# An FFT filter and a bilinear layer on one core: x's seven blocks and w_out's blocks 1024 bytes apart, used from 12 bytes behind the tile's begin

## The chip, the core and the metric

The kernel runs on one core of one Trainium2 chip. The metric is the device time of one launch in microseconds. Before the change it is 2662.38 us, the median of three runs (2661.9 to 2662.65). The profile is of one more execution, which took 2663.02 us.

A core has five engines that matter here: TensorE (PE; its weight loads are a row of their own, PEld), VectorE (DVE), ScalarE (ACT), GpSimd (POOL) and SyncE (SP), which here issues most DMAs. A matmul has a *stationary* operand, 128 x 128 weights that are loaded first, and a *moving* operand, which streams past them from SBUF, one column at a time, and gives one column of the result in PSUM each.

## The reference

x is 8 x 3072 x 256. Along the 3072 positions it is filtered in the frequency domain, and the result goes through a bilinear layer of 1536 hidden features:

```python
X = np.fft.rfft(x, axis=1)                  # 8 x 1537 x 256
Y = X * (filt_r + 1j * filt_i)[None]
y = np.fft.irfft(Y, n=3072, axis=1)         # float32
t = y.reshape(8 * 3072, 256)
a, b = t @ w_a, t @ w_b                     # 256 -> 1536 each
out = (a * b) @ w_out                       # 1536 -> 256
```

## The kernel before, in words

The FFT is done as two short transforms with a store to DRAM between them, forward and back, all as matmuls. Batch 0 goes through it in a stage of its own at the start, in an order written out by hand (FIRST). After that the kernel streams: while TensorE does the bilinear layer of batch b, the transforms of batch b+1 are put in between at places given by slots (`at(slot, ...)`). The schedule is manual; each engine runs its instructions in the order in which the code issues them.

The bilinear layer runs over 8 batches, 6 chunks of 512 tokens in each (c), and 6 pairs of hidden blocks in each chunk (p; two of the 12 blocks of 128 features). All its operands are split in a high and a low part, rounded to the float32r type, and a product is three matmuls: high weights by high x, low weights by high x, high weights by low x (L644, L645, L646 in `term`). The products a and b take Strassen's seven terms instead of eight: the chunk of x is kept as seven blocks of 256 columns (four quadrants and three sums, `x_parts`), in the tiles xoh (high) and xol (low), two buffers of each, taken in turn by the chunks. One `term` is six matmuls with one x block as the moving operand of 256 columns, and weights w as the stationary one. A pair has seven terms, 42 matmuls.

The product of a and b is made on VectorE (g), rounded on ScalarE (gh, L652), its remainder taken on GpSimd (gl, L653). `project` then multiplies it by w_out: gh and gl are the stationary operands, and a 256-column block n = 2p + f of w_out's high and low parts, woh and wol, is the moving one (L663, L664, L665). A pair has eight such triples, 24 matmuls. So a pair has 66 matmuls with an x block or a w_out block as the moving operand, and there are 8 x 6 x 6 = 288 pairs.

Where the blocks lie is what the change touches. In SBUF a block of 256 float32 takes 1024 bytes in each partition. Before, the x blocks stand XW = 261 elements (1044 bytes) apart, and the whole tile is used from 0 bytes behind its begin in even chunks and from SHIFT = 2 elements (8 bytes) in odd ones; w_out's blocks stand WW = 257 elements (1028 bytes) apart. The program that is built puts every one of these tiles at a multiple of 64 bytes. So the address at which a block begins, modulo 16 bytes, is

- x block i (0 to 6): 4 i modulo 16 in even chunks (0, 4, 8, 12, 0, 4, 8) and 4 i + 8 in odd ones (8, 12, 0, 4, 8, 12, 0);
- w_out block n: 4 n modulo 16, that is 0 or 8 for f = 0 and 4 or 12 for f = 1.

This address modulo 16 of the moving block is called its *class* below: class 0, 4, 8 or 12. Stationary operands (w, gh, gl) all begin at multiples of 64.

The blocks are written by ScalarE and GpSimd: xoh at L628, xol at L629 (four pieces of a chunk, of one or two blocks each), woh at L307, wol by the helper on L316.

Of the kernel before, what the change touches and what calls it, by code (L numbers as in the profile page):

```python
# [9 lines left out]
F32 = mybir.dt.float32  # L10
F32R = mybir.dt.float32r
# [7 lines left out]
B, S, D, DFF = 8, 3072, 256, 1536  # L19
N1, N2 = 128, 24  # L20
NB = 32
NF = DFF // 128
NP = NF // 2
NC = 6
NI = 12
NJ = 16
NFT = 4
XW, SHIFT, WW = 261, 2, 257
ODD = [1, 5, 7, 11, 13, 17, 19, 23]

PAIRS = [(0, 2), (4, 6), (8, 10), (12, 14), (16, 18), (20, 22), (3, 9), (15, 21), (1, 5), (7, 11), (13, 17), (19, 23)]
# [177 lines left out]
def fft_filter_bilinear_kernel(ctx: ExitStack, tc, x, filt_r, filt_i, wa, wb, wo, s1c, gc, fc, fl, ic, sc, s1f, ff, fi, out):  # L209
# [3 lines left out]
    def pool(name, bufs=1, space=None):  # L213
        kw = {} if space is None else {"space": space}
        return ctx.enter_context(tc.tile_pool(name=name, bufs=bufs, **kw))

    const = pool("const")
    p2 = pool("p2", 2)


    edge = ctx.enter_context(tc.tile_pool(name="edge", bufs=1, side="right"))
    few = edge.tile([128, 24], F32, name="few")
    sct, cut = few[:, 0:2], few[:, 2:4]


# [23 lines left out]
            wt[p] = const.tile([128, 4, 7, 128], F32R, name=f"w{p}")  # L249
        return wt[p]  # L250

    woh = const.tile([128, NF, WW], F32R, name="woh")[:, :, :D]
    wol = const.tile([128, NF, WW], F32R, name="wol")[:, :, :D]
    fct = const.tile([128, 3, 128], F32R, name="fct")
    flt = const.tile([96, 2, 128], F32R, name="flt")
    ict = const.tile([128, 3, 96], F32R, name="ict")
# [360 lines left out]
    def x_parts(b, c, part):  # L617
        xf = held["x", b, c]
        if part == 0:
            o = SHIFT * ((b * NC + c) % 2)  # L620
            held["xo", b, c] = [
                p2.tile([128, 7 * XW + 8], F32R, name=t, tag=t)[:, o:o + 7 * XW].rearrange("p (i w) -> p i w", w=XW)[:, :, :256]
                for t in ("xoh", "xol")
            ]
        xh, xl = held["xo", b, c]
        for o, i in (((0, 1), (0, 1)), ((1, 3), (2, 4)), ((3, 5), (4, 6)), ((5, 7), (6, 8)))[2 * part:2 * part + 2]:
            o, i = slice(*o), slice(*i)
            nc.scalar.copy(out=xh[:, o], in_=xf[:, i])  # L628
            nc.gpsimd.tensor_tensor(out=xl[:, o], in0=xf[:, i], in1=f32(xh[:, o]), op=ALU.subtract)  # L629
        if part:  # L630
            del held["x", b, c]
# [101 lines left out]
    with tc.manual_schedule():  # L733
# [21 lines left out]
        is2(0, 0, 0)  # L755
        is2(0, 0, 1)
        x_parts(0, 0, 0)
        x_parts(0, 0, 1)

        last = None  # L760
        for b in range(B):
# [5 lines left out]
            o = 0 if b else 12  # L767
# [12 lines left out]
            if b + 1 < B:  # L780
# [5 lines left out]
                for i in range(NI):  # L786

                    t = o + i if b == 0 else 2 * i
# [7 lines left out]
                t = 26 if b == 0 else 28  # L796
# [4 lines left out]
                for i in range(NJ):  # L801
                    t = 29 + 2 * i
# [8 lines left out]
            for c in range(NC):  # L811
                nb, ncx = (b, c + 1) if c + 1 < NC else (b + 1, 0)
                if nb < B:
                    t = 12 * c + 5 if c + 1 < NC else 67
                    if ncx == 0:
                        at(t - 2, load_t, nb, 0)
                    elif c == 0 and b == 0:
                        at(0, load_t, 0, 1)
                    at(t, is2, nb, ncx, 0)
                    at(t + 2, is2, nb, ncx, 1)  # L820
                    if ncx + 1 < NC:
                        at(t + 3, load_t, nb, ncx + 1)
                    at(t + 3, x_parts, nb, ncx, 0)
                    at(t + 4, x_parts, nb, ncx, 1)
# [12 lines left out]
        b, c = B - 1, NC - 1  # L837
# [38 lines left out]
```

## Time and profile before

| | |
|---|---|
| median of three runs | 2662.38 us |
| the profiled execution's own time | 2663.02 us |
| its span, first to last instruction | 2661.2 us |
| PE busy | 2597.3 us, 98% |
| DVE, ACT, POOL busy | 62%, 53%, 49% |
| granted TensorE clock, mean | 0.988 |

The profile's times count from the first instruction. A matmul's recorded duration is its way through the pipeline, and several are under way at once; how many matmuls PE gets through is read from the distance between the *start* of one and the start of the next, here called its spacing. Idle time is listed with what ended it. [...]

### The profile page before, as it was taken

What the parts mean: (1) busy time and instruction counts of PE and PEld (TensorE: products, weight loads), DVE (VectorE), ACT (ScalarE), POOL (GpSimd) and SP (SyncE); (2) the same over time, 40 slices, a digit from 0 to 9 for tenths busy, and PEclk for the clock granted to TensorE, in tenths of its full rate; (3) what the DMA queues carried; (4) which work ended last, traced back from release to release, by engine and by line L of the source; (5) the groups of instructions that cost most, each with busy time, mean ns of one, the idle gap of its engine ahead of it and who ended that gap; (6) DMA issues with size and microseconds to landing.
All of it is one profiled execution on the core that took longest, in us unless ns stands there. A gap on an engine that the chain in (4) does not pass through costs nothing.

```text
span 2661.2 us, 53762 instructions
## 1 busy us (share of the span) xinstructions
PE 2597.3 (98%) x20920; PEld 2532.3 (95%) x20920; DVE 1647.6 (62%) x2576; ACT 1413.2 (53%) x2630; POOL 1304.3 (49%) x1074
## 2 busy tenths in 40 slices
PE   6689999999999999999999999999999999999999
PEld 3389999999999999999999999999999999999999
DVE  4655885558845687457864578555884568744443
ACT  4555554555555555555555555555555555545444
POOL 3665454545544554454545444544554455434333
PEclk8799999999999999999999999999999999999999
DMA  9636441444324442244413444134432444310000
GB/s 290 182 103 229 129 131 61 138 147 147 99 76 147 146 142 90 84 156 143 139 60 127 141 148 134 60 131 147 143 107 78 133 159 137 90 35 29 29 21 17
DMA packets 213264, 312.97 MB, mean 118 GB/s; under 512 B 19872, under 2 KB 119776, under 8 KB 212960
## 3 DMA queue, kind: packets, MB, share of 16 engines
q1 hardware_dynamic: 186240, 284.09, 33.7%
q10 hardware_dynamic: 26768, 25.44, 3.2%
q8 instruction: 164, 2.69, 0.4%
q14 instruction: 92, 0.75, 0.1%
HBM read 204.59 MB, written 108.00 MB: 117 GB/s over the span
## 4 chain that ended last, share of the span: by engine, by line
PE 92%; DMA 3%; POOL 2%; DVE 1%; ACT 1%; issue 1%; SPq 0%; POOLq 0%; DVEq 0%; ACTq 0%
PE ps_p L644 10%; PE ps_p L646 10%; PE ps_p L645 10%; PE po L665 10%; PE po L664 10%; PE po L663 10%; PE ps_r L646 5%; PE ps_r L645 5%; PE ps_r L644 5%; PE ps L606 3%; PE ps_q L645 2%; PE ps_q L644 2%; PE ps_q L646 2%; PE ps L388 2%; PE ps L434 2%; PE ps L433 2%
## 5 line engine op out<-in xcount | busy, mean ns | idle before, releaser
L653 POOL TENSOR_TENSOR gl<-g,gh 128x512 fp32r<-128x512 f32 x576 | 755.3, 1311 | 996.2 <-ACT gh L652 968.5
L644 PE MATMUL ps_p<-xoh,w 128*128 128x256 f32 x2304 | 652.3, 283 | 9.8 <-ACT s L685 6.7
L663 PE MATMUL po<-woh,gh 128*128 128x256 f32 x2304 | 657.0, 285 | 0.0
L665 PE MATMUL po<-woh,gl 128*128 128x256 f32 x2304 | 649.7, 282 | 2.6 <-POOL gl L653 2.6
L646 PE MATMUL ps_p<-xol,w 128*128 128x256 f32 x2304 | 650.8, 282 | 0.0
L645 PE MATMUL ps_p<-xoh,w 128*128 128x256 f32 x2304 | 650.1, 282 | 0.0
L664 PE MATMUL po<-wol,gh 128*128 128x256 f32 x2304 | 649.6, 282 | 0.0
L652 ACT CAST gh<-g 128x512 fp32r<-128x512 f32 x576 | 358.4, 622 | 537.3 <-DVE g L711 462.5
L689 DVE TENSOR_TENSOR cs<-ps_r,s 128x512 f32<-128x512 f32 x288 | 199.1, 691 | 446.6 <-PE ps_r L646 394.2
L685 ACT COPY s<-ps_p 128x512 f32<-128x512 f32 x576 | 337.9, 587 | 248.6 <-PE ps_p L646 212.2
L644 PEld LDWEIGHTS ps_p<-xoh,w 128*128 128x128 f32 x2304 | 437.2, 190 | 11.4 <-ACT s L685 7.3
L665 PEld LDWEIGHTS po<-woh,gl 128*128 128x128 f32 x2304 | 436.6, 190 | 3.4 <-POOL gl L653 3.4
L664 PEld LDWEIGHTS po<-wol,gh 128*128 128x128 f32 x2304 | 436.9, 190 | 3.0
L663 PEld LDWEIGHTS po<-woh,gh 128*128 128x128 f32 x2304 | 436.6, 190 | 3.1
L645 PEld LDWEIGHTS ps_p<-xoh,w 128*128 128x128 f32 x2304 | 437.7, 190 | 0.0
L646 PEld LDWEIGHTS ps_p<-xol,w 128*128 128x128 f32 x2304 | 436.5, 189 | 0.3 <-POOL xol L629 0.3
L646 PE MATMUL ps_r<-xol,w 128*128 128x256 f32 x1152 | 325.8, 283 | 1.4 <-POOL xol L629 1.4
L644 PE MATMUL ps_r<-xoh,w 128*128 128x256 f32 x1152 | 324.4, 282 | 0.0
L645 PE MATMUL ps_r<-xoh,w 128*128 128x256 f32 x1152 | 324.3, 281 | 0.0
L689 DVE TENSOR_TENSOR cs<-ps_q,s 128x512 f32<-128x512 f32 x288 | 199.2, 692 | 198.7 <-PE ps_q L646 172.6
L711 DVE TENSOR_TENSOR g<-cs 128x512 f32<-128x512 f32 x288 | 294.8, 1024 | 1.7 <-POOL gl L653 1.7
L723 DVE TENSOR_TENSOR g<-ps_p,cs 128x256 f32<-128x256 f32 x288 | 122.2, 424 | 219.0 <-ACT cs L722 218.0
(98 smaller groups left out, 4529.6 us busy)
## 6 DMA issues: line engine op xcount, KB each, us to landing
filt<-in_fr SPq DMA_DIRECT2D x122, 256.0 KB, 3.1
z<-zh SPq DMA_DIRECT2D x112, 256.0 KB, 3.0
zt<-z SPq DMA_DIRECT2D x112, 256.0 KB, 2.9
td<-t ACTq DMA_DIRECT2D x128, 192.0 KB, 2.1
out<-ot SPq DMA_DIRECT2D x95, 256.0 KB, 2.0
tt<-td SPq DMA_DIRECT2D x47, 512.0 KB, 4.3
xt<-in_x SPq DMA_DIRECT2D x84, 256.0 KB, 2.8
st<-s1d SPq DMA_DIRECT2D x84, 256.0 KB, 3.0
```

What stands on the lines that cost most here:

```text
L644: nc.tensor.matmul(o, wh, xh[:, i], start=first and h == 0, stop=False, skip_group_check=True)
L645: nc.tensor.matmul(o, wl, xh[:, i], start=False, stop=False, skip_group_check=True)
L646: nc.tensor.matmul(o, wh, xl[:, i], start=False, stop=True, skip_group_check=True)
L652: nc.scalar.copy(out=gh, in_=g[:, f])
L653: nc.gpsimd.tensor_tensor(out=gl, in0=g[:, f], in1=f32(gh), op=ALU.subtract)
L663: nc.tensor.matmul(o, gh[:, ts], woh[:, n], start=n == 0 and j % 2 == 0, stop=False, skip_group_check=True)
L664: nc.tensor.matmul(o, gh[:, ts], wol[:, n], start=False, stop=False, skip_group_check=True)
L665: nc.tensor.matmul(o, gl[:, ts], woh[:, n], start=False, stop=n == NF - 1, skip_group_check=True)
L685: nc.scalar.copy(out=s, in_=bank)
L689: nc.vector.tensor_tensor(out=cs[:, :, n], in0=bank, in1=s, op=ALU.add)
L711: nc.vector.tensor_tensor(out=g[:, 0].rearrange("p (t n) -> p t n", t=2), in0=cs[:, 0, 0:2], in1=cs[:, 1, 0:2], op=ALU.mult)
L723: nc.vector.tensor_tensor(out=g[:, 1, :256], in0=ps[:, 1], in1=a21, op=ALU.mult)
```

## The change

The seven x blocks now stand 256 elements (1024 bytes) apart, w_out's blocks too, and each of the four kinds of tile (xoh, xol, woh, wol) is three elements longer than its blocks and used from the third element on, 12 bytes behind its begin, in every chunk. A small tile (`few`, four columns of constants in use) is made 16 columns shorter.

```diff
-XW, SHIFT, WW = 261, 2, 257
...
-    few = edge.tile([128, 24], F32, name="few")
+    few = edge.tile([128, 8], F32, name="few")
...
-    woh = const.tile([128, NF, WW], F32R, name="woh")[:, :, :D]
-    wol = const.tile([128, NF, WW], F32R, name="wol")[:, :, :D]
+    woh, wol = (const.tile([128, 3 + NF * D], F32R, name=t)[:, 3:].rearrange("p (n d) -> p n d", d=D) for t in ("woh", "wol"))
...
     def x_parts(b, c, part):
         xf = held["x", b, c]
         if part == 0:
-            o = SHIFT * ((b * NC + c) % 2)
             held["xo", b, c] = [
-                p2.tile([128, 7 * XW + 8], F32R, name=t, tag=t)[:, o:o + 7 * XW].rearrange("p (i w) -> p i w", w=XW)[:, :, :256]
+                p2.tile([128, 7 * 256 + 3], F32R, name=t, tag=t)[:, 3:].rearrange("p (i w) -> p i w", w=256)
                 for t in ("xoh", "xol")
             ]
```

No engine gets another instruction or another order: on each of them the same instructions stand in the same places, and only the addresses and, where two blocks are written at once, the pattern differ (two runs of 256 elements become one run of 512). In the program that is built after the change the four tiles begin at multiples of 32 bytes; so every one of the blocks begins at 12 modulo 16, in all chunks: all are of class 12. As the tiles are shorter, most other tiles lie 64 to 704 bytes lower than before, and those on the right side of SBUF 64 bytes higher; all operands of the other matmuls still begin at multiples of 16.

## Rows read from the trace of the kernel before

**Rows 1.** The page: span, busy time and share of it, instructions.
```profile
span 2661.2 us, 53762 instructions
...
PE 2597.3 (98%) x20920; PEld 2532.3 (95%) x20920; DVE 1647.6 (62%) x2576; ACT 1413.2 (53%) x2630; POOL 1304.3 (49%) x1074
```
**Rows 2.** Busy time by stage: stretch, length, busy us (instructions), clock, DMA, GB/s.
```profile
0.00:100.00 100.00, 66.26 (x146) 29.95 (x146) 56.59 (x83) 48.53 (x87) 50.48 (x64) 0.85 0.89 278
...
220.00:260.00 40.00, 38.96 (x326) 38.70 (x325) 20.31 (x37) 23.96 (x46) 23.57 (x19) 1.00 0.74 250
260.00:2640.00 2380.00, 2378.65 (x19628) 2356.05 (x19627) 1495.85 (x2334) 1272.36 (x2364) 1153.56 (x910) 1.00 0.35 109
```
**Rows 3.** Who waited for whom from 280 to 2640 us: total us, times, longest.
```profile
POOL gl L653 <- ACT gh L652: 904.3, 443, 4.4
...
PE ps_r L646 <- POOL xol L629: 1.4, 7, 0.2
```
**Rows 4.** PE's timeline, an odd chunk: start us, us, instruction.
```profile
1508.99 0.28 PE L644 MATMUL ps_p<-xoh,w 128*128 128x256 f32 x1
...
1509.69 0.28 PE L663 MATMUL po<-woh,gh 128*128 128x256 f32 x1
...
1511.13 0.28 PE L644 MATMUL ps_p<-xoh,w 128*128 128x256 f32 x1
...
1511.83 0.28 PE L388 MATMUL ps<-xh,st 128*128 128x256 f32 x1
```
**Rows 5.** PE's timeline, the even chunk behind it, the same two terms.
```profile
1517.56 0.28 PE L644 MATMUL ps_p<-xoh,w 128*128 128x256 f32 x1
...
1518.28 0.28 PE L663 MATMUL po<-woh,gh 128*128 128x256 f32 x1
...
1519.71 0.28 PE L644 MATMUL ps_p<-xoh,w 128*128 128x256 f32 x1
...
1520.43 0.28 PE L388 MATMUL ps<-xh,st 128*128 128x256 f32 x1
```
**Rows 6.** PE's timeline: first and last matmul of class 0 from 260 us on.
```profile
260.00 0.28 PE L646 MATMUL ps_p<-xol,w 128*128 128x256 f32 x1
...
2650.80 0.28 PE L646 MATMUL ps_p<-xol,w 128*128 128x256 f32 x1
```
**Rows 7.** The same of class 4.
```profile
260.48 0.28 PE L644 MATMUL ps_q<-xoh,w 128*128 128x256 f32 x1
...
2651.52 0.28 PE L665 MATMUL po<-woh,gl 128*128 128x256 f32 x1
```
**Rows 8.** The same of class 8.
```profile
262.61 0.28 PE L663 MATMUL po<-woh,gh 128*128 128x256 f32 x1
...
2655.25 0.29 PE L665 MATMUL po<-woh,gl 128*128 128x256 f32 x1
```
**Rows 9.** The same of class 12.
```profile
261.20 0.28 PE L644 MATMUL ps_r<-xoh,w 128*128 128x256 f32 x1
...
2655.85 0.28 PE L664 MATMUL po<-wol,gh 128*128 128x256 f32 x1
```
**Rows 10.** PE's timeline: first and last matmul of L388 from 260 us on.
```profile
470.22 0.28 PE L388 MATMUL ps<-xh,st 128*128 128x256 f32 x1
...
2155.99 0.28 PE L388 MATMUL ps<-xh,st 128*128 128x256 f32 x1
```
**Rows 11.** Groups by line and form, ACT and POOL: busy us, mean ns, idle before.
```profile
L653 POOL TENSOR_TENSOR gl<-g,gh 128x512 fp32r<-128x512 f32 x576 | 755.3, 1311 | 996.2 <-ACT gh L652 968.5 <-PE ps_p L646 18.8 <-PE po L665 9.0
L629 POOL TENSOR_TENSOR xol<-xf,xoh 128x512 fp32r<-128x512 f32 x144 | 179.7, 1262 | 0.1
L652 ACT CAST gh<-g 128x512 fp32r<-128x512 f32 x576 | 358.4, 622 | 537.3 <-DVE g L711 462.5 <-PE ps_p L646 30.3 <-PE ps L433 19.6
L628 ACT CAST xoh<-xf 128x512 fp32r<-128x512 f32 x144 | 84.6, 623 | 0.0
```
**Rows 12.** The chain of waits around the end of batch 0: start us, us, what.
```profile
451.20 0.13 PE ps_r L646
...
454.13 1.30 POOL gl L653
455.43 1.27 POOL xol L629
...
456.75 0.39 PE ps_r L646
```

## The prediction

> **What bounds the kernel now.** I read the page's first block, then the table by stages, then the waits, and then PE's timeline. The page shows PE busy for 98% of a span of 2661.2 us, and no other engine above 62% [rows 1]. [...]
>
> The spacing is what the timeline shows. I took every matmul of L644 to L646 and L663 to L665 that starts from 260 us on, with the start of the next matmul, and sorted them by the class of their moving block. 108 with a spacing of 135 ns or more I set aside; 90 of them stand between an L663 and its L664, at about 200 ns, two in nearly every chunk and as many in class 4 as in class 12, so I leave their excess as it is. The other 17,997 give these means (the rows are the first and the last of each class):
>
> - class 0: 118.06 ns, 4930 matmuls [rows 6]
> - class 4: 120.55 ns, 4059 [rows 7]
> - class 8: 119.95 ns, 4942 [rows 8]
> - class 12: 117.20 ns, 4066 [rows 9]
> - all: 118.95 ns
>
> One can see it with the eye. In an odd chunk the term on block 5 is of class 12 and takes from 1508.99 to 1509.69, six matmuls in 0.70 us; the term on block 6 (class 0) 0.70 us [rows 4]. In the even chunk behind it the same two terms are of class 4 and class 8 and take 0.72 us each [rows 5]. The work is the same, only the address differs. Single terms scatter by as much as that; the means over four thousand do not.
>
> **The change, part by part.**
>
> *All moving blocks become class 12.* If a matmul takes its class's spacing, 4930 gain 0.86 ns, 4059 gain 3.35 and 4942 gain 2.75: 4.2 + 13.6 + 13.6 = 31.4 us. What this takes for granted is that class 12 does the same at every place. The trace has class 12 only in odd blocks (x blocks 1, 3, 5, and f = 1), where it stands against class 4, and class 0 against class 8 only in even ones. If even places could do no better than their class 0, the gain would be 13.6 + 4942 x 1.88 ns = 9.3, so 22.9 us. That is the lower bound of this term; I take 31.4, since the low and high x parts and both w_out parts show the same order of the four classes, and so it doesn't look like a matter of the place. That class 12 borrows from its neighbours can be excluded: the 2736 matmuls of class 12 with class 12 both before and behind them have a mean of 117.15 ns [rows 9].
>
> *Before 260 us* stand another 902 such matmuls. At the same 1.75 ns each they could give 1.6 us, but part of that stage ends in other waits [rows 2]; I take half, 0.8 us.
>
> *Blocks 1024 bytes apart.* The fear is that all reads now fall on one grid. The trace has such matmuls: L388 reads blocks of 256 columns 1024 bytes apart, from class 0, and its 432 matmuls have a mean spacing of 118.5 ns [rows 10], no more than class 0 elsewhere with its odd distances. Cost 0; if it were there, it is a rival below.
>
> *The writers.* Pieces of two blocks were two runs of 256 elements, and become one run of 512. On ACT L628 with two runs takes 623 ns and L652 with one run 622; on POOL L629 takes 1262 and L653 with one run 1311 [rows 11]. So ACT gains nothing, and POOL may lose up to 0.05 us in each of 144 pieces, where it sits idle for 996 us before L653 alone [rows 11]: 0, except where PE waits for it.
>
> *The wait that stays.* At the ends of seven batches a chain goes from PE's term at 451.20 over DVE and ACT to POOL's gl and xol, and back to PE at 456.75 [rows 12]. In these 5.5 us PE does about 45 matmuls; when they are done 45 x 1.75 ns = 0.08 us earlier, the chain is not, and the wait grows by 0.08, with POOL's 0.05 at most 0.13. Seven times: 0.6 to 0.9 us. I take 0.6. Behind this matmul stands all of PE's work, so the wait costs its full length.
>
> *Tiles that lie elsewhere.* Everything else keeps its multiples of 16; of DMAs into the shifted tiles the first 100 us could feel a difference [rows 2]. No row prices it. From the spread of the three runs shown (0.75 us) and a stage of 100 us that is 0.89 full, I bound it at 2 us either way and take 0. The shorter `few` costs nothing.
>
> Sum: 31.4 + 0.8 - 0.6 = 31.6 us off. The profiled execution took 2663.02 us, so 2631.4; the median of the runs stands 0.64 us lower, so about 2631 us.
>
> [...] The rows show spacings that depend on the address, and 119 ns on the mean [rows 6 to 9]. [...]
>
> The rows also show that classes 0 and 12 are fast and 4 and 8 slow [rows 6 to 9]. [...]
>
> **The rivals.**
>
> [...]
> [...]
> 3. *No change.* The classes' difference is made up elsewhere, PE's spacing being held by its weight loads, one per matmul and busy for 95% of the span [rows 1]: 2662 us. Against it: the weights have the same addresses modulo 64 in all classes, and yet the classes differ.
> 4. *More than forecast.* Class 12 at even places lies as far under class 0 as it lies under class 4 at odd ones: another 2.5 ns for 9872 matmuls, 25 us: 2606 us. Nothing speaks for it but that it wasn't seen.
>
> **How the numbers follow.** The forecast, with its two ends (22.9 to 31.4 us in the main stage, 2 us for the start, some more for single matmuls behind each other), gets 0.73 and by itself covers 2623 to 2641 us. Rival 1 gets 0.12, rival 2 0.06, rival 3 0.05, rival 4 0.04. The range that holds 8 in 10 reaches from the forecast over rival 1: 2617 to 2650. A measurement of this kernel can tell 0.2% from no change, about 5 us. Faster: forecast and rivals 1 and 4, 0.89. Within 0.2%: rival 3, 0.05. Slower: rival 2, 0.06.
>
> **What would show it.** In the profile after, PE is as full from 260 us on, the last start comes some 31 us earlier, and the mean spacing of the six lines is 117.2 ns, the same in odd and even chunks and in odd and even blocks; even blocks at 118 would be rival 1, all above 119 rival 2, 119 with classes gone rival 3. The seven waits for xol stand at about 2 us in total instead of 1.4; if they are far above 4 us, or a new line of waits appears on PE in the main stage, the step on the writers was wrong. The first 220 us should be the same within 2 us. The prediction is wrong if the spacing doesn't fall, or falls and PE's holes take it back.

## The result, and the profile after

The changed kernel takes 2637.68 us (median of four runs, 2636.53 to 2638.26) against 2662.35 us, now the median of four runs of the kernel before: the ratio is 0.9906, with a 95% interval of 0.9891 to 0.9921. That is 24.7 us less, where 31 were forecast. Its profiled execution took 2638.26 us, with a span of 2636.5.

Line numbers fall by 2 or 3: term's L644 to L646 are now L641 to L643, project's L663 to L665 are L660 to L662, gl's L653 is L650, xol's L629 is L626. The page's first block and the two long stages of the table by stages (columns as in [rows 1, 2]) read:

```profile
span 2636.5 us, 53762 instructions
...
PE 2565.3 (97%) x20920; PEld 2495.5 (95%) x20920; DVE 1637.2 (62%) x2576; ACT 1410.5 (53%) x2630; POOL 1319.2 (50%) x1074
```
```profile
0.00:100.00 100.00, 66.05 (x146) 29.41 (x146) 57.08 (x83) 48.54 (x87) 50.62 (x64) 0.86 0.90 277
...
260.00:2614.00 2354.00, 2347.70 (x19620) 2320.70 (x19619) 1485.03 (x2334) 1268.96 (x2363) 1166.75 (x910) 1.00 0.35 110
```

The engines have the same numbers of instructions. PE's main stage is shorter, but no longer without a hole: 6.3 of 2354 us are idle, where it was 1.35 of 2380 [rows 2]. POOL is the one engine that became busier, 1319.2 us against 1304.3.

First the matmuls. These are the terms of [rows 4, 5] in PE's timeline of the changed kernel: block 5 in the odd chunk, and blocks 5 and 6 in the even one.

```profile
1497.00 0.28 PE L641 MATMUL ps_p<-xoh,w 128*128 128x256 f32 x1
...
1497.71 0.28 PE L660 MATMUL po<-woh,gh 128*128 128x256 f32 x1
...
1505.42 0.28 PE L641 MATMUL ps_p<-xoh,w 128*128 128x256 f32 x1
...
1506.11 0.28 PE L660 MATMUL po<-woh,gh 128*128 128x256 f32 x1
...
1507.51 0.28 PE L641 MATMUL ps_p<-xoh,w 128*128 128x256 f32 x1
...
1508.21 0.28 PE L386 MATMUL ps<-xh,st 128*128 128x256 f32 x1
```

The two terms that took 0.72 us in the even chunk take 0.69 and 0.70 us; the one in the odd chunk, of class 12 before and after, takes 0.71 where it took 0.70, so single terms scatter here too. Over the whole stage from 260 us on, sorted as for the prediction, 17,957 matmuls of class 12 (from 260.07 to 2631.10 us) have a mean spacing of 116.94 ns, where all classes together had 118.95. Even blocks stand at 117.04, odd ones at 116.83.

Then the waits. What PE and its weight loads waited for from POOL between 280 and 2600 us (us in total, times, longest):

```profile
PEld po L662 <- POOL gl L650: 7.9, 21, 0.4
PEld ps_r L643 <- POOL xol L626: 4.0, 7, 0.6
PE po L662 <- POOL gl L650: 2.8, 14, 0.2
PE ps_r L643 <- POOL xol L626: 2.6, 7, 0.4
```

The line for xol was there before, with 1.4 us [rows 3]; the two for gl are new, at 21 places, three in each of seven batches. The matmuls with a spacing of 135 ns or more, the ones that the means leave out, are 150 instead of 108; above 119 ns each they come to 22.5 us instead of 12.1. Of these 10.4 us, 9.1 stand at the 21 places for gl and 1.2 at the seven for xol.

Why gl is late there shows in the chain of waits from 286 us on (start us, us, what), and in POOL's groups (columns as in [rows 11]):

```profile
285.50 2.64 POOL xol L626 x2
288.14 0.03 POOL gl L650
288.17 1.17 issue
289.34 1.83 POOL xol L626 x2
291.17 1.13 issue
292.30 1.29 POOL gl L650
293.60 0.04 issue
293.64 0.38 PE po L662
```
```profile
L650 POOL TENSOR_TENSOR gl<-g,gh 128x512 fp32r<-128x512 f32 x576 | 744.8, 1293 | 964.1 <-ACT gh L649 672.0 <-PE ps_p L643 292.1
L626 POOL TENSOR_TENSOR xol<-xf,xoh 128x512 fp32r<-128x512 f32 x144 | 203.5, 1429 | 0.0
```

The chain leaves PE and runs over POOL: the pieces of xol and the second gl of a pair stand in one row there, and the 512-element pieces take 1429 ns on the mean where they took 1262 [rows 11]. (POOL is at work in the two stretches of 1.17 and 1.13 us called issue, too; its timeline stands under xf8 below.) PE reaches gl's matmul before POOL is done.

It had not been far from that before. Here is the same place in the timeline of the kernel before (start us, us, instruction):

```profile
289.42 2.36 POOL L629 TENSOR_TENSOR xol<-xf,xoh 128x512 fp32r<-128x512 f32 x2
291.74 1.75 POOL L653 TENSOR_TENSOR gl<-g,gh 128x512 fp32r<-128x512 f32 x1
293.69 0.29 PE L665 MATMUL po<-woh,gl 128*128 128x256 f32 x1
```

gl was done at 293.49 us, 0.20 us before the first matmul on it began; at all 21 places that margin was 0.17 to 0.25 us. A place with so little to spare appears in no list of waits.

The account, from the traces: 18,107 x (118.95 - 116.94) ns = 36.4 us gained by the spacing, 10.4 us lost to waits, and 0.5 us lost before 260 us (at 226 us the same matmul starts 0.47 us later than before). That is 25.5 us; the last L661 starts 24.75 us earlier than the last L664 of before, and the 0.75 us between the two were not traced.

### The profile page after: what moved, and what is told of

It reads as the page before. It is cut to its first block, busy times and chain, and to the rows that moved or that the text cites. A ratio compares the mean times of both kernels' runs of the same rounds, so it can differ in the third digit from the quotient of the medians.

```text
span 2636.5 us, 53762 instructions
## 1 busy us (share of the span) xinstructions
PE 2565.3 (97%) x20920; PEld 2495.5 (95%) x20920; DVE 1637.2 (62%) x2576; ACT 1410.5 (53%) x2630; POOL 1319.2 (50%) x1074
## 4 chain that ended last, share of the span: by engine, by line
PE 84%; POOL 6%; DMA 3%; issue 3%; DVE 2%; ACT 1%; SPq 0%; ACTq 0%; POOLq 0%; DVEq 0%
PE po L662 9%; PE ps_p L641 9%; PE po L660 9%; PE ps_p L642 9%; PE ps_p L643 9%; PE po L661 9%; PE ps_r L643 5%; PE ps_r L641 5%; PE ps_r L642 5%; PE ps L604 3%; POOL xol L626 3%; PE ps_q L641 2%; PE ps_q L642 2%; PE ps_q L643 2%; PE ps L386 2%
## 5 line engine op out<-in xcount | busy, mean ns | idle before, releaser
L650 POOL TENSOR_TENSOR gl<-g,gh 128x512 fp32r<-128x512 f32 x576 | 744.8, 1293 | 964.1 <-ACT gh L649 672.0
L660 PE MATMUL po<-woh,gh 128*128 128x256 f32 x2304 | 654.7, 284 | 0.0
L641 PE MATMUL ps_p<-xoh,w 128*128 128x256 f32 x2304 | 644.5, 280 | 10.4 <-ACT s L682 6.9
L662 PE MATMUL po<-woh,gl 128*128 128x256 f32 x2304 | 643.7, 279 | 7.0 <-POOL gl L650 6.1
L661 PE MATMUL po<-wol,gh 128*128 128x256 f32 x2304 | 643.2, 279 | 0.0
L642 PE MATMUL ps_p<-xoh,w 128*128 128x256 f32 x2304 | 643.1, 279 | 0.0
L643 PE MATMUL ps_p<-xol,w 128*128 128x256 f32 x2304 | 639.9, 278 | 0.0
L662 PEld LDWEIGHTS po<-woh,gl 128*128 128x128 f32 x2304 | 436.0, 189 | 12.1 <-POOL gl L650 12.1
L641 PEld LDWEIGHTS ps_p<-xoh,w 128*128 128x128 f32 x2304 | 432.7, 188 | 12.1 <-ACT s L682 7.7
L661 PEld LDWEIGHTS po<-wol,gh 128*128 128x128 f32 x2304 | 435.9, 189 | 3.2
L660 PEld LDWEIGHTS po<-woh,gh 128*128 128x128 f32 x2304 | 433.3, 188 | 3.0
L643 PEld LDWEIGHTS ps_p<-xol,w 128*128 128x128 f32 x2304 | 435.5, 189 | 0.3 <-POOL xol L626 0.3
L643 PE MATMUL ps_r<-xol,w 128*128 128x256 f32 x1152 | 320.9, 279 | 2.6 <-POOL xol L626 2.6
L641 PE MATMUL ps_r<-xoh,w 128*128 128x256 f32 x1152 | 322.4, 280 | 0.0
L708 DVE TENSOR_TENSOR g<-cs 128x512 f32<-128x512 f32 x288 | 301.2, 1046 | 9.6 <-POOL gl L650 9.6
L464 POOL TENSOR_TENSOR yl<-y,yh 128x512 fp32r<-128x512 f32 x112 | 144.2, 1288 | 220.3 <-ACT yh L463 220.3
```

Of the source, the lines that this page charges most:

```text
L464: nc.gpsimd.tensor_tensor(out=yl, in0=y, in1=f32(yh), op=ALU.subtract)
L641: nc.tensor.matmul(o, wh, xh[:, i], start=first and h == 0, stop=False, skip_group_check=True)
L642: nc.tensor.matmul(o, wl, xh[:, i], start=False, stop=False, skip_group_check=True)
L643: nc.tensor.matmul(o, wh, xl[:, i], start=False, stop=True, skip_group_check=True)
L650: nc.gpsimd.tensor_tensor(out=gl, in0=g[:, f], in1=f32(gh), op=ALU.subtract)
L660: nc.tensor.matmul(o, gh[:, ts], woh[:, n], start=n == 0 and j % 2 == 0, stop=False, skip_group_check=True)
```

## Experiments

Two questions: is it the offset that sets the spacing, and not the distance of 1024; and what made POOL slow, and with it the waits? For the second, a mean had hidden something. Split by the class of the block that they begin at, the 512-element pieces of before have two durations: about 1.09 us for those written to class 4 (the second of their two blocks then is of class 8), and 1.29 us for those written to class 12 (the second of class 0), with 14 of the 72 pieces of the one kind (1.28 to 1.56 us) and 20 of the 72 of the other (1.48 to 1.75 us) taking longer. xf, the other input, lies at class 0. In the changed kernel all pieces are written to class 12, and none is below 1.27 us. So POOL could be slow by where the block lies (theory D) or by how its two inputs lie to each other modulo 16 bytes: slow at 0 and 12 apart, fast at 4 and 8 (theory R).

**off0, off1, off2: the offset alone.** In each, only the offset differs from the changed kernel; sizes and buffers stay.

```diff
-    ...[:, 3:].rearrange("p (n d) -> p n d", d=D) for t in ("woh", "wol"))
+    ...[:, 0:0 + NF * D].rearrange("p (n d) -> p n d", d=D) for t in ("woh", "wol"))
...
-                p2.tile([128, 7 * 256 + 3], F32R, name=t, tag=t)[:, 3:]...
+                p2.tile([128, 7 * 256 + 3], F32R, name=t, tag=t)[:, 0:0 + 7 * 256]...
```

(`1:1` and `2:2` in the place of `0:0` in the other two.) Expected of off0:

> The changed kernel with one thing different: the four tiles are used from their begin (0 bytes) and not from 12 bytes behind it; sizes, buffers and all other addresses stay. All moving blocks are of class 0. Theory A (the class sets the spacing, and class 12 is really better than class 0): mean spacing 118.0 ns against 116.9, about 19 us of matmuls more than the changed kernel, 2655 us. [...]

Of off1:

> The changed kernel with the four tiles used from 4 bytes behind their begin: all moving blocks of class 4, all else as there. Theory A (the class sets the spacing): 120.6 ns on the mean against 116.9, 18,105 x 3.6 ns = 66 us more, less some 9 us of waits on GpSimd that a slower TensorE and faster pieces take away: about 2695 us, slower than before the change. Theory B (it is the even distance of 1024 bytes that makes it fast, not the offset): within 5 us of the changed kernel. GpSimd: the 512-element pieces of xol at 1.09 to 1.1 us instead of 1.29 and more, where nothing of VectorE holds them up.

Of off2:

> The changed kernel with the four tiles used from 8 bytes behind their begin: all moving blocks of class 8, all else as there. Theory A: 119.9 ns on the mean, 54 us of matmuls more than the changed kernel, less some 9 us of waits: about 2683 us. Theory B (the even distance): within 5 us of the changed kernel. GpSimd's 512-element pieces of xol at 1.09 to 1.1 us, as under off1.

| blocks at | time, us | ratio to before, 95% | mean spacing, ns | spacings from 135 ns on | xol's 512-element pieces, ns |
|---|---|---|---|---|---|
| mixed (before) | 2662.35 | | 118.95 | 108 | 1262 |
| 0 (off0) | 2663.86 | 1.0005 [0.9995, 1.0014] | 118.40 | 150 | 1434 |
| 4 (off1) | 2697.16 | 1.0131 [1.0115, 1.0146] | 121.01 | 108 | 1160 |
| 8 (off2) | 2689.93 | 1.0103 [1.0086, 1.012] | 120.57 | 108 | 1164 |
| 12 (the change) | 2637.68 | 0.9906 [0.9891, 0.9921] | 116.94 | 150 | 1429 |

Each ratio is to runs of the kernel before that were made beside it; their medians lie between 2662.35 and 2663.21 us. The four rows below the first all have the even distance of 1024 bytes, and they span 59 us. The order is that of the classes in the trace of before, and each level lies within 0.7 ns of its class there. The distance alone brings nothing, and class 12 is better than class 0 by 1.5 ns on the mean, in even blocks (117.04 against 118.10) and in odd ones (116.83 against 118.77). It is not better in each tile: the second xoh buffer has 118.57 ns in class 12 and 117.25 in class 0 (more on this under al64xf8). off0 was expected at 2655 and came out at 2664: its spacing was 0.4 ns above the 118.0 expected, some 7 us. It gains 10 us in spacing over before and loses 8.2 of them again, because it has the slow pieces and the waits (its long spacings come to 20.3 us above 119 ns). off1 came out 2 us above what was expected and off2 7 us above, at 120.57 ns for the 119.9 expected.

The waits from 280 to 2600 us tell the second question. Of off0:

```profile
PEld po L662 <- POOL gl L650: 5.6, 21, 0.3
PEld ps_r L643 <- POOL xol L626: 3.9, 7, 0.6
PE ps_r L643 <- POOL xol L626: 2.5, 7, 0.4
```

In off1 and off2 there is no wait for gl at all. off0's matmuls are hardly faster than those of before, and yet it waits: so the slow pieces make the waits, and the fast TensorE only makes them longer (5.6 us here, 7.9 in the changed kernel).

**xf8 and xf12: the source of the pieces moved.** The blocks stay in class 12; xf, which ScalarE and VectorE write and GpSimd subtracts from, moves by 8 bytes, or by 12 (`3:3 + 8 * 256` in the place of `2:2 + 8 * 256`).

```diff
-            held["x", b, c] = moe[0].tile([128, 8, 256], F32, name="xf", tag="xf")
+            held["x", b, c] = moe[0].tile([128, 8 * 256 + 16], F32, name="xf", tag="xf")[:, 2:2 + 8 * 256].rearrange("p (i w) -> p i w", w=256)
```

> The changed kernel with the float32 source xf of the x blocks used from 8 bytes behind its tile's begin (the tile is 64 bytes longer); the moving blocks stay in class 12. Theory R (GpSimd's price depends on how input xf and the blocks lie to each other modulo 16: slow at 0 and 12 apart, fast at 4 and 8): the 512-element pieces fall from 1.43 to about 1.1 us, most of the 21 waits for gl and part of the seven for xol go, 8 us off, about 2630 us, faster than before and after. Theory D (GpSimd is slow where the written block itself begins at 12 or 0): pieces stay at 1.43 us, the waits stay, 2638 us. Spacing 116.9 ns in both.

> xf8 with xf used from 12 bytes behind its tile's begin instead of 8, so that xf and the x blocks lie 0 apart modulo 16. Theory R: the 512-element pieces are back at 1.43 us on the mean, the 21 waits for gl too, 2637 us as in the changed kernel. If it was only the moved xf that made them fast (its own place off a multiple of 16), they stay at 1.1 to 1.2 us and the time at 2624 us. Spacing of TensorE 116.9 ns in both.

xf8: 2624.14 us (2623.46 to 2626.54), ratio 0.9856 [0.9841, 0.987]. xf12: 2637.95 us, 0.9906 [0.989, 0.9923]. The spacing is 116.93 and 116.94 ns, as in the changed kernel. The pieces' group, of xf8 and then of xf12:

```profile
L626 POOL TENSOR_TENSOR xol<-xf,xoh 128x512 fp32r<-128x512 f32 x144 | 164.9, 1159 | 1.2
```
```profile
L626 POOL TENSOR_TENSOR xol<-xf,xoh 128x512 fp32r<-128x512 f32 x144 | 203.2, 1425 | 0.0
```

And all that PE and its weight loads wait for from POOL between 280 and 2600 us, of xf8 and then of xf12:

```profile
PEld ps_r L643 <- POOL xol L626: 1.9, 7, 0.3
```
```profile
PEld po L662 <- POOL gl L650: 8.1, 21, 0.4
PEld ps_r L643 <- POOL xol L626: 3.8, 7, 0.5
PE po L662 <- POOL gl L650: 2.9, 14, 0.2
PE ps_r L643 <- POOL xol L626: 2.4, 7, 0.3
```

Theory D is out: the output is of class 12 in both. Nor is it that xf was moved: 12 bytes, which puts it 0 apart from the blocks, change nothing. With xf 4 apart the pieces are fast, the 21 waits are gone, the long spacings are back at 108, and the time falls by another 13.5 us, where 8 were expected. Between the two profiled executions it is 11.7 us, of which the long spacings account for 11.3 (11.2 us above 119 ns instead of 22.5).

POOL's timeline shows how narrow it is (start us, us, instruction), of the changed kernel and then of xf8, in the pair of the chain above:

```profile
289.34 3.00 POOL L626 TENSOR_TENSOR xol<-xf,xoh 128x512 fp32r<-128x512 f32 x2
292.30 1.28 POOL L650 TENSOR_TENSOR gl<-g,gh 128x512 fp32r<-128x512 f32 x1
```
```profile
288.94 2.14 POOL L626 TENSOR_TENSOR xol<-xf,xoh 128x512 fp32r<-128x512 f32 x2
291.04 1.74 POOL L650 TENSOR_TENSOR gl<-g,gh 128x512 fp32r<-128x512 f32 x1
```

In the changed kernel the second piece takes 1.74 us itself, in xf8 it is gl that does; in both some 0.45 us more than alone. At that time VectorE makes its sum of y (L456), which reads two tiles in SBUF: it starts at 290.50 and takes 0.69 us in the changed kernel, and starts at 290.41 and takes 1.22 us in xf8. Over the whole of the changed kernel's trace, the last piece of a chunk takes 1.74 to 1.78 us in the 21 chunks where this sum falls into its time, and 1.28 to 1.32 us in the other 27. No run here took that meeting away, so that it is the cause of the 0.45 us is not shown. In xf8 POOL comes to gl 1.26 us earlier, gl is done at 292.78 and not at 293.58, and PE doesn't notice: at the 21 places gl is now done 0.37 to 0.49 us before its first matmul.

**g8: the same for gl.** xf8, and g moved by 8 bytes too, so that gl's inputs g and gh lie 8 apart and no longer 0.

```diff
-        g = moe[0].tile([128, 2, 512], F32, name="g", tag="g")
+        g = moe[0].tile([128, 2 * 512 + 16], F32, name="g", tag="g")[:, 2:2 + 1024].rearrange("p (f n) -> p f n", f=2)
```

> xf8 with the tile g, too, used from 8 bytes behind its begin; gh and gl stay at multiples of 64, so input and output of the subtraction that makes gl lie 8 apart modulo 16, where they lay 0 apart. Theory R (GpSimd's price is set by how its operands lie to each other): gl falls from 1.29 to about 1.1 us, 576 x 0.2 = 115 us less work on GpSimd. As TensorE hardly waits for gl in xf8, the time falls by no more than 1 to 2 us: 2622 to 2624 us. Theory D (the output's own place decides): gl stays at 1.29 us, 2624 us.

2621.71 us (2619.73 to 2624.92), ratio 0.9846 [0.9832, 0.9861]. gl's group:

```profile
L650 POOL TENSOR_TENSOR gl<-g,gh 128x512 fp32r<-128x512 f32 x576 | 641.9, 1114 | 1045.5 <-ACT gh L649 689.2 <-PE ps_p L643 349.6 <-PE ps_q L643 6.6
```

Theory R holds for another instruction and another pair of tiles: 1311 ns in xf8, 1114 here, and POOL is at 45% of the span. As forecast it is worth next to nothing, since PE no longer waits for gl in this stretch; the runs of xf8 and g8 overlap, and whether the 2.4 us between their medians are real stays open.

**wonly and xonly: one half of the change.** The kernel before with the new lines for w_out's tiles alone, or for x's tiles alone.

```diff
-    woh = const.tile([128, NF, WW], F32R, name="woh")[:, :, :D]
-    wol = const.tile([128, NF, WW], F32R, name="wol")[:, :, :D]
+    woh, wol = (const.tile([128, 3 + NF * D], F32R, name=t)[:, 3:]... for t in ("woh", "wol"))
```

> The kernel before with the change made to w_out's two tiles alone (class 12 for all their blocks, 1024 bytes apart); x's blocks stay as before. The theory that the class sets the spacing and that the waits come from GpSimd's pieces of x: the 6,500 matmuls on w_out fall from 118.9 to 117.2 ns, 11 us; x's pieces on GpSimd keep their 1.1 and 1.3 us and no wait is added: 2651 us. If the waits come from a faster TensorE alone, whatever GpSimd does, some of the 21 waits for gl appear here too, and the time is some 3 us more.

> The kernel before with the change made to x's two tiles alone; w_out's blocks stay 1028 bytes apart. The theory: the 11,600 matmuls on x fall from 119.0 to about 116.8 ns, 25 us; GpSimd's 512-element pieces rise to 1.43 us and the waits for gl come, 8 to 10 us back: about 2647 us. Rival (the faster TensorE makes the waits): with a smaller part of the gain the waits are only half as large, 2643 us.

wonly: 2653.84 us, ratio 0.9965 [0.9953, 0.9977], 3 us above what was expected; its w_out matmuls have 117.20 ns, x's 119.05, and there are 108 long spacings, no wait for gl. xonly: 2651.68 us, 0.9953 [0.9937, 0.997]; x's matmuls have 117.24 ns, w_out's 118.83, with 150 long spacings and the 21 waits:

```profile
PEld po L663 <- POOL gl L651: 7.0, 21, 0.4
```

So the waits come with x's half alone, although it speeds up only two thirds of the matmuls. xonly fell short of the 2647 us expected by 5 us, mostly as its x matmuls stayed 0.4 ns above those of the changed kernel.

**d1040: class 12 without the distance of 1024.**

```diff
-    ... const.tile([128, 3 + NF * D], F32R, name=t)[:, 3:].rearrange("p (n d) -> p n d", d=D) ...
+    ... const.tile([128, 3 + NF * 260], F32R, name=t)[:, 3:].rearrange("p (n d) -> p n d", d=260)[:, :, :D] ...
...
-                p2.tile([128, 7 * 256 + 3], F32R, name=t, tag=t)[:, 3:].rearrange("p (i w) -> p i w", w=256)
+                p2.tile([128, 7 * 260 + 3], F32R, name=t, tag=t)[:, 3:].rearrange("p (i w) -> p i w", w=260)[:, :, :256]
```

> The changed kernel with all blocks 1040 bytes apart and not 1024, still from 12 bytes behind the tile's begin: every block of class 12, the places modulo 64 spread over 12, 28, 44 and 60. Theory A (the class is what counts, the distance not): 116.9 to 117.2 ns on the mean, GpSimd's pieces slow as in the changed kernel, 2638 us within 5. Theory G (the distance of 1024 brings part of the gain, since class 12 was at 117.2 in the kernel before, with odd distances): spacing above 117.2, up to 5 us slower than the changed kernel.

2636.75 us, ratio 0.9899 [0.9885, 0.9914], mean spacing 116.94 ns, 150 long ones, pieces at 1429 ns: the changed kernel again in time, mean spacing, waits and pieces. For these the distance counts for nothing, only what it makes of the address modulo 16. What it does change is how the mean is made up, which comes next.

**al64xf8: all buffers at multiples of 64.** In the changed kernel the blocks of the second xoh buffer took 118.57 ns, those of the first 116.37. The second begins 32 bytes behind a multiple of 64, the first at one.

```diff
-    ... const.tile([128, 3 + NF * D], F32R, name=t)[:, 3:] ...
+    ... const.tile([128, 16 + NF * D], F32R, name=t)[:, 3:3 + NF * D] ...
...
-                p2.tile([128, 7 * 256 + 3], F32R, name=t, tag=t)[:, 3:]...
+                p2.tile([128, 7 * 256 + 16], F32R, name=t, tag=t)[:, 3:3 + 7 * 256]...
```

> xf8 with the four tiles 52 bytes longer, so that all buffers begin at multiples of 64 bytes as they did before the change; in the changed kernel the second buffers of xoh and xol and all of wol begin 32 bytes behind one, and blocks of the second xoh buffer took 118.6 ns there against 116.4 in the first. Theory M (the begin modulo 64 matters): the second buffer falls to 116.4 and wol to 117, about 10 us off xf8, 2614 us. Theory N (the two buffers differ for another reason: odd chunks, the other operand): no change against xf8, 2624 us.

2626.41 us (2622.89 to 2628.78), ratio 0.9859 [0.9844, 0.9874], the same as xf8 within what the runs tell. The second xoh buffer did fall, to 116.95 ns, but xol's second rose from 115.75 to 118.40 and woh from 116.92 to 117.91; over all it is 117.02 against 116.93. Theory M fails as a gain. There is a finer pattern under the classes, in which one tile's gain is another's loss. By tile and buffer the means reach from 115.2 to 118.6 ns in the changed kernel, from 117.3 to 120.5 in off0 and from 117.0 to 122.2 in off1, so a single tile can lie 4 ns off the mean of its class. In d1040, where the blocks of a tile lie at four different places modulo 64, they reach only from 116.8 to 117.2, with the same mean over all. So the wide pattern goes with blocks 1024 bytes apart, and the order of the classes holds for the mean over the tiles. What sets the pattern stays open.

## Why the prediction was right, and where it missed

*What bounds the kernel* was right: PE from 260 us on, by the spacing of its matmuls. Before the change it is busy there for 2378.65 of 2380 us [rows 2] and waits for 1.4 us [rows 3], so 89% of the span is a row of matmuls without a hole. off0 to off2 move nothing but addresses, and the time follows over 59 us.

*All blocks become class 12* was right in its mechanism and too small: 36.4 us for 31.4. Class 12 does at even places what it does at odd ones (117.04 and 116.83 ns), and when all are of it the mean is a little lower still, 116.94 for 117.20 ns. The lower bound of 22.9 us, class 0's level for even places, was not needed. One reason given against that bound was misread, though: the four tiles do not all show the same order of the classes. In the trace of before xoh has 117.56 ns in class 0 and 117.65 in class 12, and 120.07 in class 8 and 120.29 in class 4; only the other three tiles have 12 ahead of 0. *Blocks 1024 bytes apart* at no cost, and *tiles that lie elsewhere* at nothing within 2 us, were right (d1040; 0.5 us). *Before 260 us* gave nothing of the 0.8 us; PE is busy for only 66.05 of the first 100 us, and the stage came out 0.5 us longer.

*The writers* is the step that failed in size. It compared two group means, 1262 and 1311 ns, and took 0.05 us as the most that a piece could lose. The 1262 was a mean over pieces of 1.09 and of 1.29 us, by class, and some held up. The change makes all of them slow, 0.2 us more for every second one, and the last piece of a chunk, never held up before, now takes 1.74 to 1.78 us in 21 of 48 chunks, beside VectorE's sum of y as shown above; so the mean became 1429. The prediction said "0, except where PE waits for it", and looked for such places only where PE waited already. The 21 places with a margin of some 0.2 us stood in the trace of before, and this term, put at nothing, cost 9.1 us.

*The wait that stays* was right in kind and small: 0.6 us were forecast at seven places, and 1.2 came there. With the 21 new places, where gl follows two pieces of xol on POOL, the waits cost 10.4 us. The prediction's own sign for this, "a new line of waits appears on PE in the main stage", is what the profile shows. With the pieces fast again (xf8) the long spacings come to 11.2 us above 119 ns, against 12.1 before the change, and the time to 2624 us, 7 us under the forecast. The forecast of 31.6 us was a sum of a gain 5 us too small and a loss 10 us too small; that it came within 7 us of the 24.7 measured is in part luck, as the smaller error made up for half of the larger.

*The rivals.* The levels of rivals 1 and 2, on which the upper end of the range and the 0.06 for slower stand, no run with blocks at 12 shows: even blocks came to 117.04 ns and not to 118, and all blocks to 116.94 and not above 119. Rival 1, in which 12 is good by its place, is excluded by off0, too: 118.40 ns at the same places. So is rival 2, in which the change makes the kernel slower: class 12, with one element ahead of the next multiple of 16 bytes, is the fastest of the four. The third (held by the weight loads) is excluded too: the loads stayed as they were, while the spacing went from 116.9 to 121.0 ns. The fourth, more than forecast, was right in sign for the spacing alone, with 5 of its 25 us.

## What to carry to other kernels

Where TensorE is full, the spacing of its matmuls is worth sorting by the address of the moving block modulo 16 bytes; here the offset alone moved the time by 2.3%, and it can be read from a trace in which several offsets stand side by side. A tile moved for one engine must be checked for every engine that reads or writes it, since GpSimd wanted here what TensorE did not (its pieces take 1160 and 1164 ns on the mean with blocks at 4 and 8 and 1429 at 12, where the matmuls have 121.01, 120.57 and 116.94), and moving the other input settled both (xf8: 1159 and 116.93 ns). Before a group's mean is used as a price, split it by what the change alters. And where a faster or slower engine is to be priced, look not only at the waits in the trace but at the margins: here results were ready 0.2 us before they were needed, and 0.2 us more for each piece turned that into waits.

## What was not expected of the hardware

- float32r matmuls of 128 x 128 by 256 columns, at a granted clock of 1.00, with all moving blocks beginning at 0, 4, 8 or 12 modulo 16 bytes: 118.4, 121.0, 120.6 and 116.9 ns from start to start, on the mean of some 18,000 (off0, off1, off2, the change). Single tiles lie up to 4 ns off these means.
- A GpSimd subtraction of 128 x 512 float32 elements, beside which VectorE makes neither the products g (L711 and L714 before, L708 and L711 after) nor the sum of y (L458, L456), takes 1.09 to 1.12 us when its second input begins 4 bytes behind the first modulo 16 (before), and 1.27 to 1.32 us when it begins 12 behind (before and the change); with 256 elements 0.64 us at 8 behind, 0.74 at 0 (before) and 0.73 to 0.74 at 12 (the change). The means of all 512-element pieces, those that take longer among them, are 1160 and 1159 ns at 4 (off1, xf8), 1164 at 8 (off2), 1434 and 1425 at 0 (off0, xf12) and 1429 at 12 (the change). That is xol; gl was run at 0 and 8 and has 1311 ns (xf8) and 1114 (g8). Which of the three operands makes the difference was not taken apart, since the second input and the output always lay in the same class; that the output alone does it is excluded.
- ScalarE's cast of the same elements shows no such difference: L625 takes 620 ns with blocks at 12 (the change), 622 or 623 with blocks at 0, 4 and 8 (off0, off1, off2), and took 623 in mixed classes [rows 11], where the pieces that begin at 4 have 623 and those at 12 622.
